# Last 128 output columns as two groups of 64, stored as two transfers of 64 partitions from two queues

## The chip, the cores and the metric

The kernel runs on one core of a Trainium2 chip. The metric is the device time of one execution in microseconds (us). Before the change its median over three runs is 233.62 us (233.54 to 234.01).

## The reference

`x` is 16 x 512 x 1024, so 8192 tokens of 1024 values; `w` is 1024 x 1024 and `b` has 1024 values, all in bf16. In each group of four consecutive rows of `w` (along the contracted dimension) and for each column, the two entries of largest magnitude are kept and the others set to zero. Then a dense product and a bias follow:

```
wg = w.reshape(G, M, D);  mag = jnp.abs(wg)            # M = 4, N = 2
order = jnp.argsort(mag, 1)
thr = jnp.take_along_axis(mag, order[:, M - N:M - N + 1, :], 1)
wp = (wg * (mag >= thr)).reshape(D, D)
return jnp.einsum("bsd,df->bsf", x, wp) + b
```

## The kernel before

The 8192 tokens are 64 tiles (NT) of 128 tokens. For each tile, TensorE multiplies eight blocks of 128 contracted values (KT = 8) into the 1024 output columns, 512 columns to a PSUM bank in fp32. VectorE (DVE) adds the bias while it moves a bank to a bf16 tile `o` in SBUF, and a DMA stores `o` to HBM.

At the start the weights are loaded, pruned and laid out, and the first twelve tiles are worked on in an order that is written out by hand (`order`, line 257), while the pieces of the pruned weights become ready. After that `batches` (lines 44 to 49) go through the other 52 tiles, 12 to 63: the tokens of a batch come transposed by one DMA (`load_nat`, line 372, issued from SP), and the loop at line 435 runs over the batches and the tiles `t` in each. Every instruction of an engine, DMA issues included, is chained in program order (`seq`, line 64), so what an engine does next is what stands next in the code.

The names that the change and the steps of the prediction touch:

- `nat` (line 236) issues one matmul for each block kt, with its load of the weights (the transposed tokens are the stationary operand). The matmuls are recorded at line 238.
- `evac` (line 396) is the addition of the bias on DVE, recorded at line 398.
- `store` (line 409) and `issue` (line 96) start a DMA from SP's queue ("sp") or ACT's ("act"). All DMA issues are recorded at line 98. `rows(t)` (line 403) gives the rows of the output for a tile.
- `psum_o` (line 59) has six banks for the sums, `outp` (line 57) ten buffers for `o`.
- `LATE` (line 43) is 5: the tiles from NT - LATE on, 59 to 62, are stored in two halves of 512 columns, each as soon as its own addition is done; the tiles before them go in one store of 256 KB (lines 455 to 458). All these stores are issued from ACT.
- The last tile, 63 (lines 442 to 447), isn't worked on in two banks side by side as the others are, but in four groups one after the other: 512, 256, 128 and 128 columns. Each group has a bank, eight matmuls, an addition and a store of its own. The stores go out alternately from SP (512 and the first 128 columns) and ACT (256 and the last 128).

Each DMA signals its end on one of eight semaphores, which are used in turn; an issue also waits until the DMA that used its semaphore before has ended. At the end of the program SP waits for the last DMAs, and then all engines are brought together (recorded at the line that closes the program, 484).

Of the kernel before, what the change touches and what calls it, by code (L numbers as in the profile page):

```python
# [10 lines left out]
def kernel(  # L11
# [8 lines left out]
    P = 128  # L20
# [7 lines left out]
    Dout = w.shape[1]  # L28
# [4 lines left out]
    FH = 512  # L33
    CW = 256
# [5 lines left out]
    NPK = 8  # L40
    LEAD = 4
    GROUPS = ((0, 5), (5, 8))
    LATE = 5
    sizes = (4, 8, 8, 8, 8, 8, 8)
    batches = []
    t0 = NPK + LEAD
# [17 lines left out]
    def seq(eng, inst):  # L64
        if eng in tails:
            tc.add_manual_dep(inst.ins, tails[eng].ins.name, NOSYNC, reason="program order")
        tails[eng] = inst
        return inst
# [22 lines left out]
    def tokens(dram, t):  # L91
        a, b_ = next(s for s in GROUPS if s[0] <= t < s[1])
        return dram[a * P:b_ * P].rearrange("(p t) k -> p t k", p=P), t - a
    bias_sb = const.tile([P, Dout], bf16)

    def issue(eng, out_, in_):
        q = nc.sync if eng == "sp" else nc.scalar
        return seq(eng, q.dma_start(out_, in_))  # L98
# [137 lines left out]
    def nat(xt, ps, c0, c1, k0=0, k1=KT, first=0, last=KT - 1, koff=0):  # L236
        for kt in range(k0, k1):
            pe(nc.tensor.matmul(ps, lhsT=xt[:, kt - koff, :], rhs=wp_nat[:, kt, c0:c1],  # L238
                                start=(kt == first), stop=(kt == last)))
# [138 lines left out]
    def load_batch(bi):  # L378
        if bi < len(batches):
            tb, nb = batches[bi]  # L380
            xnat.update(load_nat(tb, tb + nb))
# [14 lines left out]
    def evac(o, ps, c0, c1, add=None):  # L396
        if add is None:
            dve(nc.vector.tensor_tensor(o[:, c0:c1], ps, bias_sb[:, c0:c1], op=Alu.add))  # L398
        else:
            dve(nc.vector.tensor_tensor(o[:, c0:c1].rearrange("p (n c) -> p n c", n=2),  # L400
                                        ps.rearrange("p (n c) -> p n c", n=2), add, op=Alu.add))

    def rows(t):
        if t < NPK:
            ov, n = tokens(of, t)
            return ov[:, n, :]
        return of[t * P:(t + 1) * P, :]

    def store(eng, t, o, c0=0, c1=Dout):
        issue(eng, rows(t)[:, c0:c1], o[:, c0:c1])  # L410
# [24 lines left out]
    for bi, (tb, nb) in enumerate(batches):  # L435
        if bi:
            load_batch(bi + 1)
        for j in range(nb):
            t = tb + j
            xt = xnat[t]  # L440
            o = outp.tile([P, Dout], bf16, name="o")
            if t == NT - 1:
                for n, (c0, c1) in enumerate(((0, FH), (FH, FH + CW), (FH + CW, Dout - P), (Dout - P, Dout))):
                    ps = psum_o.tile([P, FH], fp32, name="ps")
                    nat(xt, ps[:, :c1 - c0], c0, c1)
                    evac(o, ps[:, :c1 - c0], c0, c1)
                    store("act" if n % 2 else "sp", t, o, c0, c1)
            else:
                pss = [psum_o.tile([P, FH], fp32, name="ps") for _ in range(2)]
                for kt in range(KT):  # L450
                    for h in range(2):
                        nat(xt, pss[h][:], h * FH, (h + 1) * FH, kt, kt + 1)
                for h in range(2):
                    evac(o, pss[h][:], h * FH, (h + 1) * FH)
                    if t >= NT - LATE:
                        store("act", t, o, h * FH, (h + 1) * FH)
                if t < NT - LATE:
                    store("act", t, o)
# [30 lines left out]
```

## Time and profile before

| what | value | where it is from |
|---|---|---|
| median of the runs | 233.62 us (233.54 to 234.01) | the three runs |
| span of the profiled execution, first to last instruction | 231.74 us | trace |
| what lies around the span, against the median | 1.88 us | the difference of the two |
| granted TensorE clock | full in every slice | page, part 2 |
| matmuls | 226.8 us busy, 98% of the span | page, part 1 |
| DVE | 107.9 us busy, 47% | page, part 1 |
| ACT and POOL | 13.3 and 17.6 us busy | page, part 1 |
| bytes written to HBM | 16.78 MB | page, part 3 |
| store of 256 KB, 59 of them | 2.7 us from issue to landing | page, part 6 |
| store of 128 KB | 1.7 us (ACT), 1.8 us (SP) | page, part 6 |
| store of 64 KB | 1.6 us | page, part 6 |
| store of 32 KB, one from each queue | 1.5 us | page, part 6 |

How to read it: one execution is profiled, and all times in it count from its first instruction. Matmuls overlap each other, so the length of one is not the step from one to the next; the step is found from a stream of them. A DMA shows twice: as an issue on its queue (SPq or ACTq, the engine's own time), and as packets on the sixteen DMA engines, of which the profile has start, length, size and queue (SP's packets are those of q1, ACT's those of q10). "Landing" is the time from the start of the issue to the last of the sixteen signals of its end. Idle time of an engine that isn't the bottleneck costs nothing.

### The profile page before, as it was taken

To read this page: it belongs to the slowest core of one execution; us is meant where nothing else is said; L and a number is where in the kernel's file an instruction comes from. 1 tells how busy PE (TensorE), PEld (TensorE's weight loads), DVE (VectorE), ACT (ScalarE), POOL (GpSimd) and SP (SyncE) were. 2 spreads that over 40 slices of the span, in tenths; PEclk is the share of its full clock that TensorE was granted. 3 is DMA by queue.
4 is the path that set the end of the run, shared out by engine and by line. 5 is a ranking of instruction groups with operands and counts; after the bars stand their busy time and mean duration, and the time that the engine had idled before them with its cause. 6 is when DMAs were issued, how large, how long until landed. Compare 5 with 4: busy or idle time off the path is not lost.

```text
span 231.7 us, 2828 instructions
## 1 busy us (share of the span) xinstructions
PE 226.8 (98%) x1139; PEld 112.3 (48%) x1158; DVE 107.9 (47%) x184; ACT 13.3 (6%) x27; POOL 17.6 (8%) x15
## 2 busy tenths in 40 slices
PE   8999999999999999999999999999999999999995
PEld 4887444544444444444444444444444444444443
DVE  4999878754334334324324424424424423423434
ACT  3665100000000000000000000000000000000000
POOL 1000199700000000000000000000000000000000
PEclk9999999999999999999999999999999999999999
DMA  6989999996399221991249821795228972122122
GB/s 190 354 208 228 211 171 271 283 254 237 136 203 295 91 93 56 243 289 48 91 99 247 242 93 53 168 272 158 77 91 180 218 190 78 60 91 84 58 88 91
DMA packets 78268, 38.19 MB, mean 165 GB/s; under 512 B 63664, under 2 KB 70576, under 8 KB 78256
## 3 DMA queue, kind: packets, MB, share of 16 engines
q1 hardware_dynamic: 67328, 20.61, 43.2%
q10 hardware_dynamic: 10928, 17.40, 21.4%
q8 instruction: 9, 0.15, 0.3%
q14 instruction: 3, 0.02, 0.0%
HBM read 3.41 MB, written 16.78 MB: 87 GB/s over the span
## 4 chain that ended last, share of the span: by engine, by line
PE 96%; DMA 1%; issue 1%; ACTq 0%; ACT 0%; DVE 0%
PE ps L238 88%; PE ps L215 6%; PE tp L238 1%; DMA x<-in_x_dram 1%; PE tp L189 1%; ACTq L98 0%; ACT xt L194 0%; DVE o L398 0%
## 5 line engine op out<-in xcount | busy, mean ns | idle before, releaser
L238 PE MATMUL ps<-wp_nat,xb 128*128 128x512 bf16 (+2 forms) x832 | 178.9, 375 | 0.8
L238 PEld LDWEIGHTS <-xb 128*128 128x128 bf16 x848 | 82.4, 98 | 97.5
L398 DVE TENSOR_TENSOR o<-ps,bias_sb 128x512 bf16<-128x512 f32 (+1 forms) x112 | 71.6, 677 | 114.3 <-PE ps L238 112.0
L394 POOL TENSOR_TENSOR st<-st,bias_sb 128x1024 f32<-128x1024 f32 x8 | 16.7, 2132 | 0.0
L215 PE MATMUL ps<-wp,xt 128*128 128x256 bf16 x128 | 14.9, 273 | 0.0
L238 PE MATMUL ps<-wp_nat,xlow 128*128 128x512 bf16 x62 | 14.0, 379 | 0.1
L215 PEld LDWEIGHTS <-xt 128*128 128x128 bf16 x128 | 12.2, 98 | 2.0 <-ACT xt L194 0.2
L400 DVE TENSOR_TENSOR o<-ps,st 128x512 bf16<-128x512 f32 x16 | 11.1, 692 | 2.8 <-PE ps L238 2.1
L238 PE MATMUL ps<-wp_nat,xlead 128*128 128x512 bf16 x47 | 11.1, 379 | 0.1
L238 PEld LDWEIGHTS <-xlow 128*128 128x128 bf16 x64 | 7.2, 112 | 6.7
L238 PEld LDWEIGHTS <-xlead 128*128 128x128 bf16 x64 | 6.3, 98 | 7.1
L255 ACT COPY st<-ps 128x512 f32<-128x512 f32 x16 | 8.6, 599 | 6.6 <-PE ps L215 4.3
L154 DVE TENSOR_TENSOR wp<-w_sb,mag 128x512 bf16<-128x512 bf16 (+2 forms) x8 | 5.4, 690 | 0.2
L154 DVE TENSOR_TENSOR mag<-mag,hi 128x512 bf16<-128x512 bf16 (+2 forms) x8 | 5.4, 690 | 0.2
L133 PE MATMUL ps<-const-bfloat16-1.0 128*128 128x128 bf16 (+1 forms) x22 | 4.0, 364 | 0.8 <-PEq L473 0.8
L164 DVE TENSOR_SCALAR mag<-w_sb 128x512 uint16<-128x512 uint16 (+2 forms) x6 | 2.7, 466 | 3.2 <-DMA w_sb<-in_w_dram 3.2
L238 PE MATMUL tp<-wp_nat,xlead 128*128 128x512 bf16 x16 | 4.1, 379 | 0.0
L133 PEld LDWEIGHTS <-const-bfloat16-1.0 128*128 128x128 bf16 x22 | 2.2, 131 | 2.4 <-issue 2.4
L154 DVE TENSOR_TENSOR hi<-mag 128x512 bf16<-128x512 bf16 (+2 forms) x7 | 3.2, 459 | 0.1
L189 PE MATMUL tp<-ident,x 128*128 128x128 bf16 x32 | 2.8, 220 | 0.5 <-DMA x<-in_x_dram 0.2
L154 DVE TENSOR_TENSOR lo<-mag 128x512 bf16<-128x512 bf16 (+2 forms) x7 | 3.2, 457 | 0.0
L194 ACT COPY xt<-tp 128x256 f32<-128x256 f32 x8 | 2.7, 380 | 3.3 <-PE tp L189 3.3
(15 smaller groups left out, 13.3 us busy)
## 6 DMA issues: line engine op xcount, KB each, us to landing
out_dram<-o ACTq DMA_DIRECT2D x59, 256.0 KB, 2.7
wp_nat<-wp SPq DMA_DIRECT2D x14, 128.0 KB, 3.2
w_sb<-in_w_dram SPq DMA_DIRECT2D x3, 512.0 KB, 6.8
out_dram<-o ACTq DMA_DIRECT2D x8, 128.0 KB, 1.7
x<-in_x_dram SPq DMA_DIRECT2D x2, 256.0 KB, 4.3
w_sb<-in_w_dram SPq DMA_DIRECT2D x1, 256.0 KB, 5.1
x<-in_x_dram ACTq DMA_DIRECT2D x1, 256.0 KB, 3.9
bias_sb<-in_b_dram SPq DMA_DIRECT2D x1, 256.0 KB, 6.9
```

The source lines that it names most:

```text
L133: pe(nc.tensor.matmul(warm_ps[:, :rep * P], lhsT=nc.const_aps.tensor(1.0, [P, P], bf16), rhs=nc.const_aps.tensor(1.0, [P, rep * P], bf16), ...
L154: dve(nc.vector.tensor_tensor(out, a, b_, op=op))
L164: dve(nc.vector.tensor_single_scalar(self.mag[:, ms, :].bitcast(u16), self.w[:, ms, :].bitcast(u16), 0x7FFF, op=Alu.bitwise_and))
L189: pe(nc.tensor.transpose(tp[:, m, :], xg[:, m, :], ident[:]))
L194: act(nc.scalar.copy(xt[:].bitcast(fp32), xpk[t].bitcast(fp32)))
L215: pe(nc.tensor.matmul(ps[:, c0 + d:c1 + d], lhsT=xpk[t][:, m, :], rhs=wp[:, g, m, c0:c1], start=(new and m == ms.start), stop=(left[(q, n) ...
L238: pe(nc.tensor.matmul(ps, lhsT=xt[:, kt - koff, :], rhs=wp_nat[:, kt, c0:c1], start=(kt == first), stop=(kt == last)))
L255: act(nc.scalar.copy(st[:, n % 2, :, :].rearrange("p t c -> p (t c)"), ps_open.pop((q, n))[:]))
L394: pool(nc.gpsimd.tensor_tensor(st[:], st[:], bias[:, :, None, :].to_broadcast([P, 2, 2, CW]), op=Alu.add))
L398: dve(nc.vector.tensor_tensor(o[:, c0:c1], ps, bias_sb[:, c0:c1], op=Alu.add))
L400: dve(nc.vector.tensor_tensor(o[:, c0:c1].rearrange("p (n c) -> p n c", n=2), ps.rearrange("p (n c) -> p n c", n=2), add, op=Alu.add))
```

## The change

The last group of 128 columns becomes two groups of 64, each with a bank, eight matmuls and an addition of its own. Neither has a store of its own: once both additions are done, the 128 columns are stored for partitions 0 to 63 by SP and for partitions 64 to 127 by ACT. The first three groups and their stores stay (SP, ACT, SP). Besides, LATE goes from 5 to 4, so that tile 59 goes out in one store of 256 KB instead of two halves.

```diff
-    LATE = 5
+    LATE = 4
...
             if t == NT - 1:
-                for n, (c0, c1) in enumerate(((0, FH), (FH, FH + CW), (FH + CW, Dout - P), (Dout - P, Dout))):
+                cuts = (0, FH, FH + CW, Dout - P, Dout - P // 2, Dout)
+                for n, (c0, c1) in enumerate(zip(cuts, cuts[1:])):
                     ps = psum_o.tile([P, FH], fp32, name="ps")
                     nat(xt, ps[:, :c1 - c0], c0, c1)
                     evac(o, ps[:, :c1 - c0], c0, c1)
-                    store("act" if n % 2 else "sp", t, o, c0, c1)
+                    if n < 3:
+                        store("act" if n % 2 else "sp", t, o, c0, c1)
+                for eng, p0 in (("sp", 0), ("act", P // 2)):
+                    issue(eng, rows(t)[p0:p0 + P // 2, Dout - P:], o[p0:p0 + P // 2, Dout - P:])
```

In the program as built, PE has sixteen matmuls of 64 columns where eight of 128 stood, DVE two additions of 64 where one of 128 stood, ACT ends with a store of 64 x 128 and SP with another; the number of DMAs is the same as before.

## The prediction

> **What bounds the kernel now.** I read the page's head and its chain of waits first, to see which engine sets the end; then the timeline of the last microseconds, because the diff touches nothing else; then the groups by form, for prices; and last the DMA answers around every place where SP and ACT issue at the same moment. The page's head and its chain:
>
> ```profile
> span 231.7 us, 2828 instructions
> PE 226.8 (98%) x1139; PEld 112.3 (48%) x1158; DVE 107.9 (47%) x184; ACT 13.3 (6%) x27; POOL 17.6 (8%) x15
> ...
> PE 96%; DMA 1%; issue 1%; ACTq 0%; ACT 0%; DVE 0%
> ```
>
> TensorE never waits for long, and nothing in front of token tile 59 is edited. So the whole effect must come out of the drain: the time from the last tile's last matmuls to the end of the span. The timeline of the last microseconds, as start, length, engine, line, operation and count:
>
> ```profile
> 228.08 1.26 SPq L98 DMA_DIRECT2D out_dram<-o  x2
> 228.23 0.74 DVE L398 TENSOR_TENSOR o<-ps,bias_sb 128x256 bf16<-128x256 f32 x2 [0.18 <-PE ps L238]
> 229.12 0.29 DVE L398 TENSOR_TENSOR o<-ps,bias_sb 128x128 bf16<-128x128 f32 x1 [0.16 <-PE ps L238]
> ```
>
> ```profile
> 229.45 0.34 ACTq L98 DMA_DIRECT2D out_dram<-o  x1
> ```
>
> The reader is to see a strict chain. The last matmul's signal comes at 229.10, the last addition runs 229.12 to 229.42, ACT issues the last store from 229.45 to 229.79. The packet records then have its first packet at 230.29 (0.84 after the issue began), its last packet ending at 230.55 and its last completion at 230.90. From there to the span's end at 231.74 there are only SP's final waits and the drains of all engines, 0.84 us that nothing in the change touches. SP's second issue (the 128 columns before the last) starts at 229.00 and ends at 229.34.
>
> **The matmuls: 8 become 16, about +0.02 us.** The timeline of PE in three short windows gives the pace of a stream of each width:
>
> ```profile
> 219.17 2.54 PE L238 MATMUL ps<-wp_nat,xb 128*128 128x512 bf16 x11
> ```
>
> ```profile
> 227.38 0.49 PE L238 MATMUL ps<-wp_nat,xb 128*128 128x256 bf16 x3
> ```
>
> ```profile
> 228.31 0.50 PE L238 MATMUL ps<-wp_nat,xb 128*128 128x128 bf16 x6
> ```
>
> Take one matmul's own length off (379, 272 and 219 ns, below) and divide by the count less one: 216, 109 and 56 ns. That is 0.415 ns a column and some 2.7 ns besides, so 64 columns would be paced at 29 ns, if the weight load keeps up. The other bound is that a load paces it, at the 56 ns that is the shortest step on record. I take 29 because two loads are seen starting almost together, where they had waited for a copy (PEld, line 215):
>
> ```profile
> 6.71 0.12 PEld L215 LDWEIGHTS <-xt 128*128 128x128 bf16 x2
> ```
>
> Each takes 0.10 us, both together 0.12: the second started some 15 ns after the first, so loads can follow each other at half of 29 ns. Then 16 x 29 = 469 ns stand where 8 x 56 = 447 stood, +22. By width the length falls 53 ns from 256 to 128 columns, so I put 64 columns at 192 ns, not 219. The last matmul starts 49 ns later and takes 27 less: the last sum is ready at 229.12, +0.02. At 56 ns a step it would be +0.42.
>
> By the Trainium skill (TensorE: Matmul & The Clock Gate, Back-to-back issue gap) matmuls of up to 64 columns meet a floor of about 25 ns, or of about 62 ns each where the sequencer decodes in software; no run here shows 64 columns, and the 56 ns steps above lie under 62. By 25 ns the 16 would take 0.40 us, by 62 ns 0.99, which would speak against the change by half a microsecond.
>
> **The additions: -0.07 us.** The groups by form over the last 5.7 us (busy, mean ns of one):
>
> ```profile
> L398 DVE TENSOR_TENSOR o<-ps,bias_sb 128x512 bf16<-128x512 f32 x3 | 2.0, 688 | 2.8 <-PE ps L238 2.8
> L238 PE MATMUL ps<-wp_nat,xb 128*128 128x512 bf16 x7 | 1.7, 379 | 0.0
> L238 PE MATMUL ps<-wp_nat,xb 128*128 128x128 bf16 x16 | 1.1, 219 | 0.0
> L238 PE MATMUL ps<-wp_nat,xb 128*128 128x256 bf16 x8 | 1.0, 272 | 0.0
> L398 DVE TENSOR_TENSOR o<-ps,bias_sb 128x128 bf16<-128x128 f32 x2 | 0.6, 291 | 0.2 <-PE ps L238 0.2
> L398 DVE TENSOR_TENSOR o<-ps,bias_sb 128x256 bf16<-128x256 f32 x1 | 0.4, 424 | 0.2 <-PE ps L238 0.2
> ```
>
> 128 to 256 columns cost 133 ns, so 64 columns cost 291 - 67 = 224 ns. The first of the two has its sums at 228.89, inside the addition before it (228.68 to 228.97), so it starts between 228.91 and 228.97 and ends by 229.19 at the latest. It then lies beside the second group of matmuls and costs nothing; without that cover it would be 0.22. The second starts at 229.15 (or 229.19 if the two may not overlap) and ends at 229.37 (229.42), where the addition now ends at 229.42. I take 229.37: **-0.05** with the matmuls' +0.02 in it.
>
> **The two stores.** ACT waits for nothing else, so it issues at 229.40. SP cannot: it is in its own previous issue until 229.34, and that store is not moved. On the page's DMA part SP also has one more wait, for the semaphore that it reuses; in the trace of before such a wait event comes about 0.05 after an issue's end, and the next issue follows some 0.04 after it. So SP issues at about 229.45, just where ACT's only store is issued now. Behind SP's waiting store stand only its final waits, which need that store anyway. The store that ends last is therefore SP's, and it has no head start from the shorter addition.
>
> Half the partitions means 64 packets of 256 B instead of 128. The store of now keeps the engines busy for 0.26 (230.29 to 230.55), 8 packets on each of 16; 4 on each would take 0.13. That is the gain, if the two stores don't hinder each other. Against it stand the two places where both queues issue together, in the DMA answers for their moments (the last number is us to landing):
>
> ```profile
> w_sb<-in_w_dram SPq DMA_DIRECT2D x1, 64.0 KB, 2.1
> w_sb<-in_w_dram ACTq DMA_DIRECT2D x1, 64.0 KB, 2.3
> ```
>
> ```profile
> wp_nat<-wp SPq DMA_DIRECT2D x1, 128.0 KB, 2.8
> wp_nat<-wp ACTq DMA_DIRECT2D x1, 128.0 KB, 3.7
> ```
>
> At 0.73 us both queues issue 128 packets each, 4 ns apart; by the packet records the second queue's first packet comes 0.24 after the first's (2.00 against 1.76). At 23.12 the second's comes 0.79 after (25.11 against 24.32), in a busier stretch with other issues behind. So a second issuer is served behind the first, as if one unit made the packets of both. The cost of a second store of 64 packets is between nothing and 0.79; I take half of 0.24 for half the packets, 0.12, since the load at 0.73 has the same plain shape and nothing behind it. ACT's first packet is then at 229.40 + 0.84 = 230.24, SP's at 230.36, its last ends at 230.51, and the completion 0.35 later, as now, at 230.86 against 230.90. **-0.04.**
>
> The Trainium skill (DMA: Bandwidth & Descriptors, Issuing engines are not separate DMA queues) says that DMAs issued from several engines run on the same 16 engines, and that issuing from more of them saves only the issuing time. The two rows above agree in kind; by the rule the change could gain no more than part of one 0.34 issue.
>
> **Tile 59's store** goes out once, 256 KB, in place of two halves. Its additions end near 216.4, its landing takes 2.7 us by the page's row, and its buffer isn't used again: 12 us of matmuls hide it. ACT has one issue of 0.34 less there, some three microseconds ahead of its next one. The number of DMAs stays the same, so the semaphores that the last ones reuse were freed by stores issued 9 us earlier. Nothing. Without that cover it would be one landing, 2.7.
>
> **The sum.** -0.04 on the profiled span of 231.74, which lies 1.88 under the median of 233.62; I leave that distance as it is: 233.58, so **233.6**. About 0.2% (0.47 us, also the spread of the three runs shown) is what a measurement of this kernel can tell from no change.
>
> **Rivals.**
> 1. *The halves run freely beside each other.* For it: half the packets, and SP's issue of 229.00 came only 0.31 after ACT's of 228.69 without lengthening (0.34 each). Then SP's last packet is at 229.45 + 0.84 + 0.13 = 230.42 and it lands at 230.77, -0.13; if the issue of 64 also takes half of 0.34, another -0.17. Time 233.3 to 233.5. Against it: both pairs above.
> 2. *The second store waits for the first* (slower). Its place is between SP's issue and its first packet, its price what the pair at 23.12 paid: first packet 0.79 after ACT's, at 231.03, landing at 231.53, +0.63, so 234.25; at half that price, +0.24, 233.9. It decides against the change from a delay of 0.16 on, and passes 0.2% from about 0.63 on. Against it: the pair at 0.73 paid 0.24 for twice the packets.
> 3. *Weight loads pace the narrow matmuls*, 56 ns a step: +0.35 at the end of the additions (229.77), the stores as I have them: 234.0. Against it: the loads 15 ns apart. With rival 2 it would be 234.4 or more.
> 4. *The change doesn't do what it says*: the stores never run at once, as SP is held by its own earlier issue. That is half in my sum already; if ACT's is through entirely by then, the time is rival 1's.
>
> **How the numbers follow.** Forecast 0.52, rival 1 with 4 0.16, rival 2 0.22, rival 3 0.07, anything else 0.03. The range goes from rival 1's best, 233.3, less 0.1 for the scatter of a median, to rival 2's full price: 233.2 to 234.25. Over 0.2% slower: about half of rival 2, some of rival 3 and of what I don't see, and a little scatter, 0.20. Over 0.2% faster: no case reaches it by its terms, only rival 1's best end with scatter, 0.11. Within: 0.69.
>
> **What would show it.** In the profile after: 16 matmuls of 128x64 in a stream of about 0.45 us less one length (rival 3: 0.85); two additions of about 0.22; the last ending at 229.37 relative to the same last 512-column matmuls; ACT's issue 0.02 to 0.03 behind it and SP's about 0.05 behind ACT's; SP's landing about 1.4 after its issue (1.3 or less in rival 1, 1.6 to 2.1 in rival 2). I am wrong if either store's issue or landing grows, if the steps are over 40 ns, or if the steady stretch moves, which nothing here explains.

## The result, and the profile after

The changed kernel takes 234.53 us (median of seven runs, 234.15 to 234.66); the kernel before, run beside it, 233.82. The ratio is 1.0025 with a 95% interval of 1.0016 to 1.0035: slower by about 0.6 us (0.4 to 0.8; the two medians are 0.71 apart), just over the 0.2% that was to be told from no change. The prediction had 233.6, no change, with a range up to 234.25.

The page of the kernel after, head and chain:

```profile
span 232.5 us, 2864 instructions
PE 227.6 (98%) x1166; PEld 112.1 (48%) x1166; DVE 108.0 (46%) x185; ACT 13.3 (6%) x27; POOL 17.6 (8%) x15
...
PE 96%; DMA 1%; DVE 0%; ACTq 0%; ACT 0%; issue 0%
```

TensorE still makes 96% of the chain. (Some matmul records were missing in the profile before, so its count was smaller.) The span is 232.45 against 231.74, 0.71 more. Of this 0.15 lies ahead of all that was edited: the first transposes on TensorE start at 5.15 instead of 5.00, when their `x` lands, and the shift is still there at the addition of the last 512 columns (starts 227.51 against 227.36). In the thirteen profiles of this document that addition starts anywhere from 227.36 to 228.15, and the first transposes from 4.98 to 5.59. The start isn't all of it: in e7, the kernel before once more, the transposes start at 4.99 and the addition at 227.78. That is the scatter of this kernel, and it arises early: counted back from the last 512-column addition, the one 181.30 us ahead of it (at about 46 us) lies at the same distance to within 2 ns in all thirteen. So the long stretch in the middle is equal, whatever was done to the stores in it, and the other 0.56 lies behind that last 512-column addition.

The timeline of the last microseconds after, then the same two issues apart:

```profile
229.07 0.46 DVE L398 TENSOR_TENSOR o<-ps,bias_sb 128x64 bf16<-128x64 f32 x2
229.15 1.00 SPq L98 DMA_DIRECT2D out_dram<-o  x2
```

```profile
229.56 0.56 ACTq L98 DMA_DIRECT2D out_dram<-o  x1
229.59 0.56 SPq L98 DMA_DIRECT2D out_dram<-o  x1
```

The additions end at 229.52; less the shift of 0.15 that is 229.37, the predicted moment. ACT issues at 229.56 and SP at 229.59, also as predicted. But each issue takes 0.56 us, where the one of before took 0.34. The DMA answer for this stretch, us to landing at the end:

```profile
out_dram<-o SPq DMA_DIRECT2D x1, 32.0 KB, 1.5
out_dram<-o ACTq DMA_DIRECT2D x1, 16.0 KB, 1.8
out_dram<-o SPq DMA_DIRECT2D x1, 16.0 KB, 2.0
```

Half of the bytes take 1.8 and 2.0 us to land; the 32 KB of the store before them, of 128 partitions, took 1.5 as ever. The busy shares of the DMA engines in windows cut around the packets show where the time is. Of these lines only the window, its length and, at the end, clock, DMA share and GB/s matter. First before, then after:

```profile
229.45:229.82 0.37, 0.00 (x0) 0.00 (x0) 0.00 (x0) 0.00 (x0) 0.00 (x0) 1.00 0.59 169
230.12:230.28 0.16, 0.00 (x0) 0.00 (x0) 0.00 (x0) 0.00 (x0) 0.00 (x0) 1.00 0.00 0
230.28:230.56 0.28, 0.00 (x0) 0.00 (x0) 0.00 (x0) 0.00 (x0) 0.00 (x0) 1.00 0.55 117
```

```profile
229.56:229.92 0.36, 0.00 (x0) 0.00 (x0) 0.00 (x0) 0.00 (x0) 0.00 (x0) 1.00 0.55 155
230.30:230.76 0.46, 0.00 (x0) 0.00 (x0) 0.00 (x0) 0.00 (x0) 0.00 (x0) 1.00 0.00 0
230.76:231.00 0.24, 0.00 (x0) 0.00 (x0) 0.00 (x0) 0.00 (x0) 0.00 (x0) 1.00 0.38 69
231.03:231.28 0.25, 0.00 (x0) 0.00 (x0) 0.00 (x0) 0.00 (x0) 0.00 (x0) 1.00 0.36 66
```

Between the store ahead of the last and the last one the engines have nothing to do for the 0.16 us of the window before and the 0.46 of the window after; then come two short bursts one behind the other, ACT's and SP's, where before there was one. Counted from the start of the last 512-column addition, so that the shift in front drops out:

| us after that start | before | after | difference |
|---|---|---|---|
| last addition ends | 2.06 | 2.01 | -0.05 |
| ACT issues | 2.09 | 2.04 | -0.05 |
| ACT's first packet, behind its issue | 0.84 | 1.22 | +0.37 |
| SP's first packet, behind ACT's | no such store | 0.27 | +0.27 |
| packets of the last store, first start to last end | 0.26 | 0.23 | -0.03 |
| last packet's end to last signal | 0.35 | 0.35 | 0 |
| last signal | 3.54 | 4.11 | +0.56 |

The last signal to the end of the span is 0.84 in both.

### The profile page after: what moved, and what is told of

It reads as the page before. It is cut to its first block, busy times and chain, and to the rows that moved or that the text cites. A ratio compares the mean times of both kernels' runs of the same rounds, so it can differ in the third digit from the quotient of the medians.

```text
span 232.5 us, 2864 instructions
## 1 busy us (share of the span) xinstructions
PE 227.6 (98%) x1166; PEld 112.1 (48%) x1166; DVE 108.0 (46%) x185; ACT 13.3 (6%) x27; POOL 17.6 (8%) x15
## 4 chain that ended last, share of the span: by engine, by line
PE 96%; DMA 1%; DVE 0%; ACTq 0%; ACT 0%; issue 0%
PE ps L238 87%; PE ps L215 6%; PE tp L238 1%; DMA x<-in_x_dram 1%; PE tp L189 1%; DVE o L398 0%; ACTq L98 0%; ACT xt L194 0%
## 5 line engine op out<-in xcount | busy, mean ns | idle before, releaser
L398 DVE TENSOR_TENSOR o<-ps,bias_sb 128x512 bf16<-128x512 f32 (+2 forms) x113 | 71.6, 672 | 113.8 <-PE ps L238 113.7
```

## The experiments

Theory A (shape): a store of 64 partitions is slow to start, whatever the other queue does. Theory B (crowd): two issues started together slow each other. A third possibility is that something else in the edit costs: the narrow groups, or LATE. The tail, below, is the time from the end of the last addition to the last signal: 1.49 us in the kernel before, 2.10 in the changed one.

**The narrow groups with one store (e1).**

```diff
-                for eng, p0 in (("sp", 0), ("act", P // 2)):
-                    issue(eng, rows(t)[p0:p0 + P // 2, Dout - P:], o[p0:p0 + P // 2, Dout - P:])
+                store("act", t, o, Dout - P, Dout)
```

> The two groups of 64 columns and their two additions stay, LATE stays 4, but the last 128 columns go out in one store of 128 partitions from ACT. Theory A (shape): a store of 64 partitions costs more than one of 128, its issue 0.56 us instead of 0.34 and its first packet 1.2 after the issue's start instead of 0.84, whatever the other queue does. Theory B (crowd): two issues started together lengthen each other. Both expect here an issue of 0.34 us, a first packet 0.84 after it, 1.49 us from the end of the last addition to the last signal as in the kernel before, and the time of the kernel before less 0.05 (233.5 to 233.9, ratio 0.998 to 1.001). If the narrow groups themselves were the loss, the time would be 0.3 or more over the kernel before.

Ratio 1.0010 (1.0001 to 1.0019). In the profile the issue is 0.34, the first packet comes after 0.84, the additions end 2.01 after the start of the last 512-column addition, and the tail is 1.53. The stores were the loss. The time is still a little over the kernel before, though its last signal comes at 3.54 after the start of that addition, as there; e8 looks at that again.

**Two stores of full height at once (e2).**

```diff
-                for eng, p0 in (("sp", 0), ("act", P // 2)):
-                    issue(eng, rows(t)[p0:p0 + P // 2, Dout - P:], o[p0:p0 + P // 2, Dout - P:])
+                for eng, c0 in (("sp", Dout - P), ("act", Dout - P // 2)):
+                    store(eng, t, o, c0, c0 + P // 2)
```

> As the changed kernel, but the two last stores are of all 128 partitions and 64 columns each (128 packets of 128 bytes each), still issued together from SP and ACT. Theory A (shape): issues of 0.34 to 0.42 us, as for the two queues at 0.73 us in the kernel before; first packets at 0.84 to 1.0 and up to 0.24 later for the second; 1.5 to 1.75 us from the end of the last addition to the last signal; ratio to the kernel before 1.000 to 1.001. Theory B (crowd): issues of 0.5 or more on both queues, 2.0 us or more in the tail, ratio 1.002 to 1.003 as in the changed kernel.

Ratio 1.0016 (1.0007 to 1.0025), tail 1.69. The two issues in the timeline, then their landings:

```profile
229.88 0.37 ACTq L98 DMA_DIRECT2D out_dram<-o  x1
229.91 0.40 SPq L98 DMA_DIRECT2D out_dram<-o  x1
```

```profile
out_dram<-o ACTq DMA_DIRECT2D x1, 16.0 KB, 1.5
out_dram<-o SPq DMA_DIRECT2D x1, 16.0 KB, 1.6
```

The same bytes, from the same two queues, 0.03 us apart as in the changed kernel, but 128 partitions each: issues of 0.37 and 0.40, and SP's first packet 0.08 behind ACT's. Meeting lengthens an issue by 0.03 to 0.06; it doesn't make 0.56 of 0.34. B can't be the main cause. A small loss of the crowd is there, 0.2 in the tail against the kernel before and 0.16 against e1. Against the kernel before, SP's first packet comes 0.11 later after the last addition, and the last signal 0.48 instead of 0.35 after the last packet.

**Both halves from one queue (e3).**

```diff
-                for eng, p0 in (("sp", 0), ("act", P // 2)):
-                    issue(eng, rows(t)[p0:p0 + P // 2, Dout - P:], o[p0:p0 + P // 2, Dout - P:])
+                for p0 in (0, P // 2):
+                    issue("act", rows(t)[p0:p0 + P // 2, Dout - P:], o[p0:p0 + P // 2, Dout - P:])
```

> As the changed kernel, but both stores of 64 partitions are issued from ACT, one after the other, so that no other queue issues beside them. Theory A (shape): both issues 0.56 us all the same, first packet of the first 1.2 after its start, and the second lands 0.6 us later than the first: 2.4 us from the end of the last addition to the last signal, ratio to the kernel before 1.003 to 1.005. Theory B (crowd): issues of 0.34 us or less, first packet at 0.84, 1.7 to 1.8 us in the tail, ratio 1.000 to 1.002.

Ratio 1.0040 (1.0025 to 1.0054), tail 2.48. Nobody issues beside ACT:

```profile
229.58 1.22 ACTq L98 DMA_DIRECT2D out_dram<-o  x2
```

```profile
out_dram<-o ACTq DMA_DIRECT2D x2, 16.0 KB, 1.8
```

Two issues in 1.22 us (0.57 and 0.60), the first packet 1.22 after the first one's start, each landing after 1.8. This is A as expected, number by number.

**One group of 128, stored in halves (e4).** The other part of the change undone:

```diff
-                cuts = (0, FH, FH + CW, Dout - P, Dout - P // 2, Dout)
+                cuts = (0, FH, FH + CW, Dout - P, Dout)
```

> One group of 128 columns with one addition as in the kernel before, but stored as two transfers of 64 partitions from SP and ACT: the stores of the change alone (and LATE 4). Theories A and B both expect what the changed kernel shows after its last addition (2.1 us to the last signal, issues of 0.56), and the last addition ending 0.05 later than there: ratio to the kernel before 1.0025 to 1.0035. If the loss were in the narrow groups or in a meeting of both parts, the tail would be 1.5 to 1.7 us and the ratio under 1.001.

Ratio 1.0032 (1.0020 to 1.0045), tail 2.08:

```profile
229.49 0.55 SPq L98 DMA_DIRECT2D out_dram<-o  x1
229.50 0.59 ACTq L98 DMA_DIRECT2D out_dram<-o  x1
```

Issues of 0.55 and 0.59, and here ACT's first packet is the second, 0.27 behind SP's. The stores alone bring the whole loss, and one wide addition ends 0.05 later than two narrow ones (2.06 against 2.01).

**Shapes in the open (e5).** The stores of eight tiles are cut by a table, in a stretch that TensorE covers:

```diff
                 if t < NT - LATE:
-                    store("act", t, o)
+                    for eng, p0, p1, c0, c1 in probe.get(t, (("act", 0, P, 0, Dout),)):
+                        issue(eng, rows(t)[p0:p1, c0:c1], o[p0:p1, c0:c1])
```

> The kernel before, with the stores of the tiles 51 to 58 cut in other ways, in a stretch where SP's loads are over and TensorE has seconds of cover (3.45 us a tile), so that only the issues and first packets are of interest: 51 as four stores of 32 partitions from ACT, 52 as two of 64, 53 as 96 and 32, 54 as 112 and 16, 55 as two of 128 partitions and 512 columns (all from ACT), 56 as 64 from SP and 64 from ACT together, 57 as two of 128 partitions and 512 columns from SP and ACT together, 58 as 64 partitions x 128 columns twice and the rest at 128 partitions (ACT). Theory A (shape): every store of fewer than 128 partitions has an issue of about 0.56 us, alone or beside another, those of 128 partitions 0.34 (up to 0.42 together). Theory B (crowd): 0.34 or less for all that are issued from ACT alone, 0.5 or more for the issues of 56 and 57. The time stays within 0.1% of the kernel before by both.

One run, 234.51, 0.2% over the 233.97 of the kernel before beside it and more than the 0.1% expected; its profile differs from the one before in the scatter at the start (0.45) and behind the last signal (1.07 in place of 0.84), not in the middle stretch or the tail (1.50). The first issue of four tiles, ACT alone, from four windows of the timeline: 32 partitions, 64, 96, 112.

```profile
189.21 0.35 ACTq L98 DMA_DIRECT2D out_dram<-o  x1
...
192.66 0.56 ACTq L98 DMA_DIRECT2D out_dram<-o  x1
...
196.11 0.32 ACTq L98 DMA_DIRECT2D out_dram<-o  x1
...
199.57 0.32 ACTq L98 DMA_DIRECT2D out_dram<-o  x1
```

And the DMA share from the start of the issue to the first packet and just after, for 64 partitions (192.66) and for 96 (196.11):

```profile
192.66:193.85 1.19, 1.19 (x7) 0.58 (x6) 0.00 (x0) 0.00 (x0) 0.00 (x0) 1.00 0.00 0
193.85:194.35 0.50, 0.50 (x4) 0.20 (x2) 0.00 (x0) 0.00 (x0) 0.00 (x0) 1.00 0.90 197
196.11:196.91 0.80, 0.80 (x5) 0.39 (x4) 0.00 (x0) 0.00 (x0) 0.00 (x0) 1.00 0.00 0
196.91:197.41 0.50, 0.50 (x5) 0.21 (x3) 0.00 (x0) 0.00 (x0) 0.00 (x0) 1.00 0.93 242
```

64 partitions: nothing moves for 1.2 us. 96, more bytes from the same idle queue: 0.8. So A falls in its first form: not every store of fewer than 128 partitions is slow, 32, 96 and 112 aren't. A row of 128 columns on 64 partitions (tile 58) took 0.47 and 1.13 to its first packet, so row length isn't it either. Tile 56's pair of 64 had 0.55 (SP) and 0.50 (ACT), and SP's first packet came 0.61 behind ACT's. Tile 57's pair didn't meet, since SP's half waits for one addition only; it says nothing on B. The theory was then: 64 partitions in particular.

**LATE alone (e6).**

```diff
-    LATE = 5
+    LATE = 4
```

> The kernel before with LATE 4 alone: tile 59 goes out in one store of 256 KB. Both theories expect no difference (ratio 0.999 to 1.001), since the store lands some 10 us before the last one; if the tile's store mattered, the ratio would be 1.002.

Medians 233.94 and 233.97; ratio 1.0016 (0.9996 to 1.0035), the interval wide because two of its twelve executions took 235.8 and 235.9. No effect shown by the times, and none on the matmuls by the profiles: from the second addition of tile 58 to the last 512-column addition it takes 15.148 us in the kernel before, 15.148 in e6 and 15.147 in the changed kernel.

**The kernel before against itself (e7),** without any edit.

> The kernel before, unchanged, timed against itself: how far two equal programs come apart here. Every theory expects a ratio whose interval holds 1, and a last store of 128 partitions with an issue of 0.34 and a landing of 1.45 to 1.51 us.

1.0001 (0.9992 to 1.0010), tail 1.49. Ratios within 0.1% of 1 mean nothing here.

**The narrow groups alone, with LATE 5 (e8):** e1's edit on `LATE = 5`.

> The narrow groups and their two additions alone: one last store of 128 partitions from ACT, and LATE 5 as in the kernel before. By the profiles so far the tail is 0.05 us shorter than with one group of 128, so a ratio of 0.999 to 1.001. If the narrow groups cost something that the tail doesn't show (the run with LATE 4 came out at 1.0010), the ratio is again 1.0005 or more; if that was tile 59's store, it is 1.000 or less.

1.0003 (0.9993 to 1.0013), tail 1.49, the last signal 3.50 after the start of the last 512-column addition instead of 3.54. So in this profile the narrow groups gain 0.04 us, too little for the timing to tell; in e1 the last signal came 0.40 instead of 0.35 after the last packet, which took the same gain away. That e1 came out at 1.0010 isn't explained, but its interval overlaps those of e7 and e8; its last 512-column addition started at 228.15, the latest of all profiles.

**96 and 32 in place of 64 and 64 (e9).**

```diff
-                for eng, p0 in (("sp", 0), ("act", P // 2)):
-                    issue(eng, rows(t)[p0:p0 + P // 2, Dout - P:], o[p0:p0 + P // 2, Dout - P:])
+                for eng, p0, p1 in (("sp", 0, 96), ("act", 96, P)):
+                    issue(eng, rows(t)[p0:p1, Dout - P:], o[p0:p1, Dout - P:])
```

> As the changed kernel, but the last 128 columns go out as 96 partitions from SP and 32 from ACT. Theory A in its first form (any store of fewer than 128 partitions is slow): issues of 0.56 us, 2.0 us or more from the last addition to the last signal, ratio 1.0025. Theory A as the run of shapes left it (64 partitions are slow, 32, 96 and 112 aren't): issues of 0.32 to 0.44 us, first packets at 0.83 to 0.95, 1.5 to 1.7 us in the tail as for two stores of full height, ratio 1.000 to 1.0015. Theory B (crowd alone) expects 0.5 or more for both issues.

1.0008 (0.9998 to 1.0017), tail 1.67, SP's first packet 0.04 behind ACT's. The timeline:

```profile
229.75 0.40 ACTq L98 DMA_DIRECT2D out_dram<-o  x1
229.78 0.40 SPq L98 DMA_DIRECT2D out_dram<-o  x1
```

The same edit with another split, and 0.42 of the 0.61 us that the tail had grown are gone. What is left, 0.19, is about what the crowd cost in e2.

**More shapes (e10),** by e5's table:

```
51: 48 | 80    52: 80 | 48    53: 32..95 | 0..31 | 96..127    54: 64 x 512 columns, twice | 128 x 512
55: 16 | 112   56: SP 96 with ACT 32    57: 72 | 56    58: SP 64 | SP 64
```

> The kernel before, with the stores of the tiles 51 to 58 cut in other ways again; of each tile the first store is the one that starts on an idle queue. 51: 48 partitions, then 80. 52: 80, then 48. 53: 64 partitions from 32 to 95, then 32 and 32. 54: 64 partitions x 512 columns twice, then 128 partitions. 55: 16, then 112. 56: 96 from SP and 32 from ACT together. 57: 72, then 56. 58: 64 and 64, both from SP. If 64 partitions are slow as such, the first store of 53, 54 and 58 has an issue of 0.47 to 0.57 us and a first packet at 1.1 to 1.2, whatever its start, its row length and its queue, and the first stores of 51, 52, 55 and 57 have 0.35 us or less and 0.82 to 0.86. If instead the bytes or the first partition matter, 54 or 53 come out like the others.

One run, 233.84. The first issues of 51 (48 partitions), 53 (64, from 32), 54 (64, half rows) and 58 (64, from SP):

```profile
188.90 0.35 ACTq L98 DMA_DIRECT2D out_dram<-o  x1
...
195.80 0.65 ACTq L98 DMA_DIRECT2D out_dram<-o  x1
...
198.66 0.54 ACTq L98 DMA_DIRECT2D out_dram<-o  x1
...
213.06 0.56 SPq L98 DMA_DIRECT2D out_dram<-o  x1
```

64 is slow from another first partition, with half the bytes and from SP too: first packets after 1.31, 1.20 and 1.21. 16, 48 and 80 are quick (0.32 to 0.35, first packet 0.82 to 0.85). 72 had a long issue, 0.55, against the expectation, but its first packet came at 0.79: a long issue and a late first packet don't always go together. Tile 56's pair, issued in the same moment, had issues of 0.38; the first packet of SP's 96 came after 0.88, that of ACT's 32 after 1.10, 0.23 behind. So with rows of 2 KB the second queue of a 96 and 32 pair is held up far more than the 0.04 of e9.

**More counts (e11),** by the same table.

> The kernel before, with the stores of the tiles 51 to 58 cut by other counts of partitions, all from ACT; of each tile the first starts on an idle queue: 8 (then 120), 24 (then 104), 40 (then 88), 56 (then 72), 64 (then 32 and 32), 32 (then 32 and 64), 104 (then 24), and 128 partitions x 512 columns twice. 64 partitions were slow in every run so far and 72 were in one; 16, 32, 48, 80, 96, 112 and 128 were not. If all multiples of 16 but 64 are quick and the others slow, 8, 24, 40, 56 and 104 have issues of 0.5 us or more; if 64 and what lies just over it are a band of their own, they have 0.32 to 0.35. The first 64 has 0.54 to 0.65 us by both. And 32 partitions twice, one after the other, against 64 once (56 against 55): 0.35 plus 0.43 of issue against 0.56, first packet at 0.85 against 1.2.

One run, 234.24. 24, 40, 56 and 104 have issues of 0.29 to 0.33; 8 has 0.54; the first packets of all five come after 0.78 to 0.81. The DMA share for 64 partitions (issued at 203.07) and 32 (206.52):

```profile
203.07:204.27 1.20, 1.20 (x7) 0.57 (x6) 0.00 (x0) 0.00 (x0) 0.00 (x0) 1.00 0.00 0
204.27:204.57 0.30, 0.30 (x4) 0.10 (x2) 0.00 (x0) 0.00 (x0) 0.00 (x0) 1.00 0.97 218
206.52:207.32 0.80, 0.80 (x5) 0.38 (x4) 0.00 (x0) 0.00 (x0) 0.00 (x0) 1.00 0.00 0
207.32:207.62 0.30, 0.30 (x3) 0.13 (x2) 0.00 (x0) 0.00 (x0) 0.00 (x0) 1.00 0.84 198
```

32 twice against 64 once came out as expected: issues of 0.32 and 0.43 with the first packet after 0.83, against 0.56 and 1.22.

Of fourteen counts tried on an idle queue in e5, e10 and e11 only 64 has its first packet late, in each of its seven tries; most of the others were tried once. Neither guess of the expectation held: it is no rule of multiples of 16, and no band that reaches to 56. Why 64 is apart stays open.

## Why the prediction was wrong, step by step

- **The bound, and where the effect can lie.** Right: the difference is in the drain. The shift in front is scatter, and the middle stretch is equal.
- **The matmuls, +0.02.** Right. The stream of 64 columns after:

```profile
228.66 0.37 PE L238 MATMUL ps<-wp_nat,xb 128*128 128x64 bf16 x7
```

  (0.367 - 0.193) / 6 = 29 ns a step (0.367 is the line's 0.37 in full), the 29 that was taken from the wider streams. Rival 3 is out. The Trainium skill (TensorE: Matmul & The Clock Gate, Back-to-back issue gap) gives a floor of about 25 ns up to 64 columns, or 62 with hardware decode off. The 29 measured here lies above the first and under the second. The page's formula for the gap of a single matmul at full clock, N/2.4 + 2.5 ns, gives an estimate of 29.2 at 64.
- **The additions, -0.07, and -0.05 at their end.** Right, both by length and by moment. The groups by form after:

```profile
L238 PE MATMUL ps<-wp_nat,xb 128*128 128x64 bf16 x16 | 0.6, 193 | 0.0
...
L398 DVE TENSOR_TENSOR o<-ps,bias_sb 128x64 bf16<-128x64 f32 x2 | 0.4, 224 | 0.0
```

- **When the stores are issued.** Right: 229.40 for ACT and about 229.45 for SP became, less the shift, 229.40 and 229.43.
- **"ACT's first packet is then at 229.40 + 0.84".** This is the step that failed. The 0.84 was the row of a store of 128 partitions, carried over to 64 without a bound above. Measured: 1.22, +0.37, and the issue 0.56 in place of 0.34. The trace of before had a row for a transfer that doesn't run over 128 partitions on both sides: the spreads of the pruned weights, read from 32 partitions, where SP's at 23.12 has an issue of 0.54 us and its first packet after 1.20. It was used for the crowd only. As a bound above it would have come close, 1.20 against 1.22; it isn't an explanation, since stores from 32 partitions turned out quick.
- **The second store, 0.12 behind the first.** That the second starts later was right, the size wrong: 0.27 in the changed kernel and in e4. For stores of full height it is 0.08 (e2), for 96 and 32 0.04 (e9); with rows of 2 KB it is 0.61 for 64 and 64 (e5) and 0.23 for 96 and 32 (e10). So the size depends on the partitions and on the row, and half of the packets didn't mean half of the delay. That one unit makes the packets of both isn't shown.
- **The gain of half the packets.** Almost nothing came of it: 0.23 us from first to last instead of 0.26, not 0.13. 64 packets took nearly as long as 128, and the 32 of ACT in e9 still 0.19, so the count per engine isn't what spaced them. There is a slip in the sum here too: 230.36 and 0.13 make 230.49, not 230.51, so by its own terms the prediction was -0.06 and not -0.04.
- **Tile 59's store.** Nothing, as predicted: the profiles of e6 and of the changed kernel show the same 15.15 us from the last addition of tile 58 to the last 512-column addition as before.
- **The rivals.** Rival 2, the second store behind the first, is what happened in kind, with 0.27 of the 0.56. The larger part, 0.37, was in no rival. With -0.05 and -0.03 the terms sum to 0.56, inside the measured 0.4 to 0.8. Against the prediction's own -0.06 that is 0.62 more: 0.37 in the start of a store of 64 partitions, 0.15 in the second store and 0.10 in the packets.

The Trainium skill (DMA: Bandwidth & Descriptors, Issuing engines are not separate DMA queues) says that issuing from several engines saves no more than issuing time. e2 and e9 agree and go further: two queues at once cost 0.16 to 0.2 us in the tail against one store.

## What to carry to other kernels

Take the price of a transfer from a row of its own shape; a smaller one isn't cheaper by default, and where no row has the shape, put a bound above as well as below. At the end of this kernel little of the last store's latency is the moving of data: of 1.45 us from issue to last signal, 0.26 are packets, so splitting it over two queues has little to win and a second start to lose. Where such a split is wanted, try another count of partitions first: 96 and 32, with rows of 256 bytes, lengthened the tail by a third of what 64 and 64 did here.

## What the runs showed of the hardware

- Stores from SBUF to HBM of 64 partitions have issues of 0.47 to 0.65 us and first packets 1.13 to 1.31 after the issue's start (1.45 to 1.76 for the second of two queues that start together), on either queue, from first partitions 0, 32 and 64, with rows of 256 bytes to 2 KB. Stores of 8, 16, 24, 32, 40, 48, 56, 72, 80, 96, 104, 112 and 128 partitions, alone on an idle queue, have first packets after 0.78 to 0.86, and issues of 0.29 to 0.37 but for 8 and 72 (0.54 and 0.55). The cause isn't known.
- Packets of 2 KB from 64 partitions took 0.156 us each in tile 52 of e5 (median), 0.14 to 0.15 from 32 (e5, e11), and 0.084 to 0.086 from 96, 112 and 128.
- A store right behind another on one queue can have a longer issue: 32 partitions 0.43 to 0.44 behind 32, against 0.35 and 0.32 on an idle queue (e5, e11). Not always: 120 behind 8 and 88 behind 40 had 0.35 (e11), 56 behind 72 0.33 (e10).
- The last 0.84 us of the span were 0.89 to 0.90 in the profiles of e1, e2, e4 and e6 and 1.00 to 1.07 in those of e5, e10 and e11, and 0.83 to 0.84 in the others; why isn't known.
